# Moving attention visits and value copies inside a fused attention and feed-forward kernel

## The chip, the cores and the metric

The kernel runs on one core of one Trainium2 chip. The metric is the device time in microseconds (us) of one execution. Engines: PE is TensorE (matmuls), DVE is VectorE, ACT is ScalarE, POOL is GpSimd, SP is SyncE, which queues most DMAs here (155 of the 277 issues listed in the trace before). A DMA is a transfer of data that is issued to a queue; PSUM is the memory that this kernel's matmuls write to, in the banks that its plans name. A profile is one traced execution; its times count from the span's start, and the span is 1.7 us shorter than the device time of the same run. The granted clock is the share of TensorE's full speed that the profile shows as granted (1.00 is full). A wait or an idle time is "recorded" when the profile lists it between the end of one instruction and the start of the next.

## The reference

Eight batches of windowed attention (8 heads, 576 positions, width 64, each position sees 32 neighbours on either side), then a feed-forward block (FFN) on the joined heads, token by token.

```python
# attention: q, k, v of (8, 8, 576, 64)
scores = scale * np.matmul(q, k.transpose(0, 1, 3, 2))
mask = np.abs(pos[:, None] - pos[None, :]) <= 32
scores = np.where(mask, scores, -1e9)
attn = softmax(scores)                      # written out in the reference
out = np.matmul(attn, v)
# FFN on x of (4608, 512), w_in (512, 2048), w_out (2048, 512)
h = x @ w_in
g = gelu_tanh(h)
return g @ w_out
```

## The kernel before: the parts that matter

The 4608 tokens are nine blocks of 512. Block t's FFN has a first half (`x @ w_in`, GELU on ACT) and a second half (`g @ w_out`). During the second half, the attention of batch t+1 is slipped between the matmuls: a plan says before which of the matmuls which visit is queued. In a plan, `s` is scores plus exponential, `m` the mask, `v` the weighing of the values (sums `d` and outputs `o`), `x` the normalizing that writes the FFN's input; the digit is a group of two heads (-1: the tail of the batch before, that is its last group) and `@0`, `@1` pick a pair of PSUM banks, where otherwise the banks O and D are used.

```python
PLAN = {4: "s0@0 s1@1 v-1", 26: "m0 x-1", 33: "m1", 34: "s2@0 v0 v1@1", 50: "m2 x0", 56: "x1",
        62: "s3@0 v2", 82: "m3 x2", 91: "s4@1 v3", 105: "m4", 112: "x3"}

def score(b, g, pair):
    ...                                           # matmuls into ps
    pe = ap_.tile([128, 2, w], FP16, name="pe", tag="pe") if g < 4 else ...   # pool of 2 tiles
    nc.scalar.activation(pe, ps[:, :, 0:w], AF.Exp, scale=SCALE)

def mask(b, g, ...):
    nc.vector.tensor_tensor(pe, pe, band..., op=ALU.mult)
def invert(b, g, o, d):                           # 1/d on ACT as exp(-ln d)
    ...
def spread(b, g, o, lt):
    nc.vector.tensor_tensor(xT[...], o[...], lt[...], op=ALU.mult)

def pair_v(b, copy, hs=slice(0, H)):              # values also on the other 64 partitions
    V = Vs[b % 2]
    copy(V[64:128, 4:8, hs, :], V[64:128, 0:4, hs, :])
    copy(V[0:64, 4:7, hs, :], V[0:64, 1:4, hs, :])
```

From block 1 on, the second half is a Winograd product: seven products of 16 matmuls of 256 columns. After each 16, DVE copies or adds the result, and by the program a later product that accumulates in the same bank comes after that (no such wait of PE is recorded in the trace before):

```python
if n == 0:   nc.vector.tensor_copy(M1, py)
elif n == 1: nc.vector.tensor_tensor(U2, py, M1, op=ALU.add)
...
```

DVE runs its instructions in the order in which they are queued (in block 4 a mask whose input was ready at 181.60 us started at 183.65, after the addition queued before it). It also forms four weight differences (`combine`, 1.2 us each): two late in block 0 (`c` in its plan), two in block 1 at matmuls 17 and 33. Batch 2's values are copied by `pair_v` with a DMA from GpSimd's queue, and batch 1's by GpSimd itself.

The softmax here doesn't subtract the row's maximum and nothing guards it: scores larger than these inputs give would overflow.

## Time and profile before

| | before |
|---|---|
| device time, median of 3 runs | 320.15 us (319.9 to 321.78) |
| span of the profiled execution | 317.5 us |
| PE busy | 294.2 us |
| start of block 1's FFN | 62.2 us |
| block 1, start to start of block 2 | 37.6 us |
| blocks 2 to 6 together | 159.6 us |
| rest (blocks 7 and 8) | 58.1 us |

The stages are read from the timeline of PE: an FFN's first half begins where matmuls with `w_in` begin. PE is recorded as busy 93% of the span, so the places to look at are the few where PE waits. The prediction shows those lines.

### The profile page before, as it was taken

What the parts mean: (1) busy time and instruction counts of PE and PEld (TensorE: products, weight loads), DVE (VectorE), ACT (ScalarE), POOL (GpSimd) and SP (SyncE); (2) the same over time, 40 slices, a digit from 0 to 9 for tenths busy, and PEclk for the clock granted to TensorE, in tenths of its full rate; (3) what the DMA queues carried; (4) which work ended last, traced back from release to release, by engine and by line L of the source; (5) the groups of instructions that cost most, each with busy time, mean ns of one, the idle gap of its engine ahead of it and who ended that gap; (6) DMA issues with size and microseconds to landing.
All of it is one profiled execution on the core that took longest, in us unless ns stands there. A gap on an engine that the chain in (4) does not pass through costs nothing.

```text
span 317.5 us, 7161 instructions
## 1 busy us (share of the span) xinstructions
PE 294.2 (93%) x2883; PEld 184.0 (58%) x2883; DVE 191.2 (60%) x421; ACT 185.1 (58%) x283; POOL 109.2 (34%) x169
## 2 busy tenths in 40 slices
PE   6779997999499998999999999999999999999994
PEld 2444543446376467646764676467646764684483
DVE  4674585695648655865576567756775653542352
ACT  1557555567255786478647864786478647805600
POOL 3657459172405800480049004810340033007000
PEclk9989999999789999999999999999999999999998
DMA  6999998989995999399969994999392013004013
GB/s 200 249 351 368 378 316 235 247 132 143 250 170 137 181 228 200 107 148 179 242 140 182 205 213 115 176 200 224 77 213 53 2 34 102 2 0 132 2 33 99
DMA packets 117407, 52.90 MB, mean 167 GB/s; under 512 B 97935, under 2 KB 109967, under 8 KB 117374
## 3 DMA queue, kind: packets, MB, share of 16 engines
q1 hardware_dynamic: 84617, 39.66, 55.6%
q0 software_dynamic: 31824, 11.61, 30.3%
q10 hardware_dynamic: 933, 1.18, 1.1%
q8 instruction: 22, 0.36, 0.5%
q14 instruction: 11, 0.09, 0.1%
HBM read 36.70 MB, written 9.44 MB: 145 GB/s over the span
## 4 chain that ended last, share of the span: by engine, by line
PE 61%; DMA 17%; DVE 8%; ACT 5%; SPq 5%; POOL 2%; issue 1%; DVEq 0%; POOLq 0%
PE mm L544 24%; PE mm L449 16%; PE ph L449 13%; DMA wst<-in_moe_w_in_dram 3%; DMA vr<-in_v_dram 3%; DMA KT<-k 3%; DMA V<-V 3%; DMA qr<-in_q_dram 2%; DVE pe L369 2%; PE mm L515 2%; DMA V<-in_v_dram 2%; ACT pe L363 2%; PE ps_o L388 2%; SPq L133 2%; SPq L142 2%
## 5 line engine op out<-in xcount | busy, mean ns | idle before, releaser
L449 PEld LDWEIGHTS <-w_in 128*128 128x128 f16 x576 | 56.1, 98 | 66.2 <-issue 1.4
L505 POOL DMA_DIRECT2D out_dram<-y x77 | 46.3, 609 | 122.0 <-DVE y L573 121.5
L449 PE MATMUL mm<-xT,w_in 128*128 128x512 f16 x320 | 78.0, 379 | 0.2 <-DVE xT L411 0.2
L457 ACT ACTIVATE gT<-mm 128x512 f16<-128x512 f32 x80 | 47.6, 599 | 44.8 <-PE mm L449 44.2
L449 PE MATMUL ph<-xT,w_in 128*128 128x512 f16 x256 | 64.1, 379 | 0.7 <-ACT gT L457 0.7
L489 DVE TENSOR_TENSOR s<-gT 128x512 f16<-128x512 f16 x64 | 26.9, 420 | 45.4 <-ACT gT L457 45.4
L544 PEld LDWEIGHTS <-s 128*128 128x128 f16 x512 | 49.6, 98 | 6.0
L363 ACT ACTIVATE pe<-ps_s 128x960 f16<-128x960 f32 (+1 forms) x32 | 30.6, 976 | 37.7 <-PE ps_s L355 20.8
L544 PE MATMUL mm<-t,s 128*128 128x256 f16 x376 | 44.7, 273 | 0.0
L457 ACT ACTIVATE gT<-ph 128x512 f16<-128x512 f32 x64 | 36.2, 602 | 12.5 <-PE ph L449 12.4
L544 PEld LDWEIGHTS <-gT 128*128 128x128 f16 x384 | 36.7, 100 | 7.2
L544 PE MATMUL mm<-w_out,gT 128*128 128x256 f16 x256 | 34.2, 281 | 0.0
L402 ACT ACTIVATE lt<-lt 128x480 f32<-128x480 f32 (+3 forms) x40 | 23.5, 587 | 1.3
L388 PEld LDWEIGHTS <-V 128*64 128x64 f16 x520 | 15.5, 115 | 13.1 <-issue 5.9
L172 POOL DMA_DIRECT2D V<-in_v_dram x24 | 22.2, 949 | 1.2 <-DMA out_dram<-y 1.2
L89 ACT ACT_TABLE_LOAD x17 | 21.8, 1283 | 1.1 <-PEq L797 0.8
L369 DVE TENSOR_TENSOR pe<-pe,band 128x960 f16<-128x960 f16 (+1 forms) x32 | 21.7, 679 | 1.0 <-ACT pe L363 1.0
L401 ACT ACTIVATE lt<-ps_d 128x480 f32<-128x480 f32 (+3 forms) x32 | 17.5, 548 | 4.2 <-PE ps_d L382 3.8
L559 DVE COPY y<-mm 128x512 f32<-128x512 f32 x8 | 5.5, 691 | 20.3 <-PE mm L544 20.3
L515 PE MATMUL mm<-w_out,gT 128*128 128x512 f16 x64 | 15.6, 380 | 1.5 <-DVE yo L519 1.2
L544 PE MATMUL mm<-t,gT 128*128 128x256 f16 x128 | 16.3, 273 | 0.0
L355 PE MATMUL ps_s<-QT,KT 64*64 64x128 f16 (+3 forms) x648 | 14.9, 215 | 1.5 <-DVE KT L297 0.7
(85 smaller groups left out, 303.2 us busy)
## 6 DMA issues: line engine op xcount, KB each, us to landing
kr<-in_k_dram SPq DMA_DIRECT2D x32, 256.0 KB, 5.3
qr<-in_q_dram SPq DMA_DIRECT2D x6, 1024.0 KB
wst<-in_moe_w_in_dram SPq DMA_DIRECT2D x3, 1024.0 KB, 12.6
wst<-in_moe_w_out_dram SPq DMA_DIRECT2D x3, 1024.0 KB
V<-in_v_dram POOLq DMA_DIRECT2D x24, 128.0 KB, 7.1
qr<-in_q_dram SPq DMA_DIRECT2D x8, 256.0 KB
vr<-in_v_dram SPq DMA_DIRECT2D x16, 128.0 KB, 5.7
V<-V SPq DMA_DIRECT2D x5, 256.0 KB
```

The lines of the kernel that those rows point to most:

```text
L89: nc.scalar.add_instruction(mybir.InstLoadActFuncSet(name=nc.get_next_instruction_name(), act_func_set_id=which, ins=[], outs=[]))
L172: nc.gpsimd.dma_start(V[:, c, :, :], v[b, :, 128 * c:128 * c + 128, :].rearrange("h p d -> p h d"))
L363: nc.scalar.activation(pe, ps[:, :, 0:w], AF.Exp, scale=SCALE)
L369: nc.vector.tensor_tensor(pe, pe, m.rearrange("k (o j) p -> k o j p", o=1).broadcast_to(list(pe.shape)), op=ALU.mult)
L388: nc.tensor.matmul(o[64 * h:64 * h + 64, cols].rearrange("d (j p) -> d j p", j=4)[:, :, p0 - q0:p1 - q0], Vs[b % 2][:, slot, 2 * pr + h, : ...
L402: nc.scalar.activation(lt[:, 0:n], lt[:, 0:n], AF.Exp, scale=-1.0)
L449: nc.tensor.matmul(ph, w_in16[:, dc, fc * 128:fc * 128 + 128], xT[:, dc, t * 512 % RING:t * 512 % RING + 512], start=(dc == 0), stop=(dc = ...
L457: nc.scalar.activation(gTs[t][:, fc, :], phs[fc], AF.Gelu_apprx_tanh)
L489: nc.vector.tensor_tensor(dst, x, y, op=op)
L505: (eng or turn_about[0] if t == NT - 1 else eng or nc.gpsimd).dma_start(out_v[b, j, q0 + p:q0 + p + e, cols], yo[m:m + e, cols])
L515: nc.tensor.matmul(pys[t4], gTs[0][:, fc, t4 * 128:t4 * 128 + 128], w_out16[:, fc, :], start=new, stop=(fc == NF - 1))
L544: nc.tensor.matmul(pys["apart"][:, 0:256] if apart else py[:, blk, :], lhsT, wino[w][:, f, :], start=(new and i % (8 if one else 16) == 0) ...
```

## The change

The intent: let masks and normalizings run on DVE before the output additions they used to queue behind, so that PE finds them ready; take the value copies of batches 1 and 2 from GpSimd and from a DMA to DVE; keep a third tile for the exponentials; and reorder the first attention (before block 0), where PE waits 1.49 and 0.46 us for DVE's copies of the values. Cut to its core:

```diff
-PLAN = {4: "s0@0 s1@1 v-1", 26: "m0 x-1", 33: "m1", 34: "s2@0 v0 v1@1", 50: "m2 x0", 56: "x1",
-        62: "s3@0 v2", 82: "m3 x2", 91: "s4@1 v3", 105: "m4", 112: "x3"}
+PLAN = {4: "s0@0 s1@1 v-1", 16: "m0 m1 x-1", 33: "s2@0 v0@1 v1", 36: "m2", 44: "x0", 50: "x1",
+        62: "s3@0 v2", 66: "m3", 75: "x2", 91: "s4@1 v3", 105: "m4", 112: "x3"}
-PLAN_0 = {0: "w0 w1 m0", 10: "s-1@0 s1@1", 15: "m-1", 16: "w2 m1", 20: "s2@1 v-1 v0@0", 24: "w3 x-1 x0 m2", ...
+PLAN_0 = {0: "w0 w1 m0", 10: "s1@1 s-1@0", 14: "m1", 16: "w2 m-1", 18: "s2@1 v-1", 24: "w3 m2",
+          28: "d0 x-1", 31: "s3@1 v0@0", 36: "d1", 38: "m3 x0 d2", 41: "v1 v2@1", 45: "d3", 48: "x1 t4", ...
+    pep = ctx.enter_context(tc.tile_pool(name="pep", bufs=3))     # tiles of the exponentials
...   # head: values of heads 6, 7 loaded and cast before the first half weight
...   # first attention: scores of all groups earlier, weighings later, dummy matmuls moved
-                        pair_v(1, nc.gpsimd.tensor_copy, ...)     # batch 1, on GpSimd
+                elif kind == "d":                                 # batch 1, on VectorE
+                    pair_v(b, nc.vector.tensor_copy, slice(2 * g, 2 * g + 2))
-                    trans_tails(1, <bank pair S1>)
+                    trans_tails(1, <bank O>)                      # kind "t"
-        if t == 1:
-            pair_v(unpaired.pop(), nc.gpsimd.dma_start)           # batch 2, a DMA
+            if t == 1 and i == 20:
+                pair_v(unpaired.pop(0), nc.vector.tensor_copy)    # batch 2, on VectorE
```

(Output tiles of block 0 rearranged to make room.) In block 0's plan, `w` is a cast of a quarter of w_out, `d` the value copy of one pair of heads, `t` the transposes of batch 1's tails.

More of the change, by code (lines that the diff above doesn't have):

```diff
@@ L42 @@
         ("S1", "T1", True), ("A22", "T4", False), ("S4", "B22", False)]
-PLAN = {4: "s0@0 s1@1 v-1", 26: "m0 x-1", 33: "m1", 34: "s2@0 v0 v1@1", 50: "m2 x0", 56: "x1",
-        62: "s3@0 v2", 82: "m3 x2", 91: "s4@1 v3", 105: "m4", 112: "x3"}
+PLAN = {4: "s0@0 s1@1 v-1", 16: "m0 m1 x-1", 33: "s2@0 v0@1 v1", 36: "m2", 44: "x0", 50: "x1",
+        62: "s3@0 v2", 66: "m3", 75: "x2", 91: "s4@1 v3", 105: "m4", 112: "x3"}
 TURN_0 = {10: 0, 12: 1, 14: 2, 15: 3}
-PLAN_0 = {0: "w0 w1 m0", 10: "s-1@0 s1@1", 15: "m-1", 16: "w2 m1", 20: "s2@1 v-1 v0@0", 24: "w3 x-1 x0 m2",
-          30: "s3@1 v1", 36: "m3 x1", 42: "v2 v3@0", 48: "t4 x2", 51: "x3 c1", 56: "s4@1", 57: "c2 m4"}
+PLAN_0 = {0: "w0 w1 m0", 10: "s1@1 s-1@0", 14: "m1", 16: "w2 m-1", 18: "s2@1 v-1", 24: "w3 m2",
+          28: "d0 x-1", 31: "s3@1 v0@0", 36: "d1", 38: "m3 x0 d2", 41: "v1 v2@1", 45: "d3", 48: "x1 t4",
+          50: "x2", 51: "v3@0", 53: "c1", 57: "x3", 58: "s4@1", 59: "c2 m4"}
 ORDER_0 = ([(t4, 4 * w + i) for w in range(4) for t4 in (0, 1)
@@ L99 @@
     stage = ctx.enter_context(tc.tile_pool(name="stage", bufs=5))
-    yp = ctx.enter_context(tc.tile_pool(name="yp", bufs=3))
+    yp = ctx.enter_context(tc.tile_pool(name="yp", bufs=2))
     psM = ctx.enter_context(tc.tile_pool(name="psM", bufs=1, space=PSUM))
@@ L209 @@
     vs(4, 5)
+    vs(6, 7)
     wi = [load_w_in(0, stage_w(), 0, 2)]
-    vs(6, 7)
     load_w_in(0, wi[0], 2, 4)
@@ L217, with spin @@
     nc.vector.memset(idle, 0.0)
-    def spin(n, width, score=False):
-        ps = psS.tile([128, 2, 512], FP32, name="spin2", tag="S0")[:, 0, :] if score else \
+    def spin(n, width, pair=None):
+        ps = psS.tile([128, 2, 512], FP32, name="spin2", tag=f"S{pair}")[:, 0, :] if pair is not None else \
             psO.tile([128, 512], FP32, name="spin", tag="O")
@@ L312, in cast_and_turn @@
         qr, kr, qt, kt = raws[b]
-        qt16 = hp.tile([16, NPAIR, 4, 2, 64], FP16, name="qt16")
+        qt16 = hp.tile([16, NPAIR, 4, 2, 64], FP16, name="qt16", tag="qt16")
         kt16 = hp.tile([64, NPAIR, 2, 64], FP16, name="kt16", tag="t16")
@@ L360, in score @@
         w = 4 * n * len(prs)
-        pe = ap_.tile([128, 2, w], FP16, name="pe", tag="pe") if g < 4 else \
+        pe = pep.tile([128, 2, w], FP16, name="pe", tag="pe") if g < 4 else \
             tailp.tile([128, 2, w], FP16, name="pet")
@@ L517, in ffn_out_0 @@
         if fc == NF - 1:
-            yo = yp.tile([128, 512], FP32, name="yo", tag="yo")
+            if t4 == 0:
+                pys["yo"] = hp.tile([128, 2, 512], FP32, name="yo2", tag="qt16")
+            yo = pys["yo"][:, t4, :] if t4 < 2 else yp.tile([128, 512], FP32, name="yo", tag="yo")
             nc.vector.tensor_copy(yo, pys[t4])
@@ L601 @@
     cast_v(0, 2)
+    cast_v(0, 3)
     cast_w(wi[0], w_in16[:, :, 0:512], 0, (0, 1))
-    cast_v(0, 3)
     cast_w(wi[0], w_in16[:, :, 0:512], 0, (2, 3))
@@ L625 @@
     score(0, 0, 0)
-    spin(2, 512)
+    spin(2, 512, 1)
     pt = turn(1)
@@ L629 @@
     mask(0, 0)
-    spin(4, 512)
+    spin(4, 512, 1)
     score(0, 1, 1)
-    cast_vt(0)
-    spin(2, 512)
     pt = turn(2)
     trans_out(0, 2, pt)
+    cast_vt(0)
+    mask(0, 1)
+    spin(4, 512, 0)
+    score(0, 2, 0)
     paired(0)
-    mask(0, 1)
+    spin(3, 512, 1)
     weighed(0)
-    score(0, 2, 0)
+    mask(0, 2)
+    pt = turn(3)
+    trans_out(0, 3, pt)
     spread(0, 0, *ods[0])
-    spin(5, 512)
+    spin(4, 512, 1)
+    score(0, 3, 1)
     paired(1)
+    spin(2, 512, 0)
     weighed(1)
-    pt = turn(3)
     paired(2)
-    trans_out(0, 3, pt)
-    mask(0, 2)
-    spin(3, 512, score=True)
-    score(0, 3, 1)
+    mask(0, 3)
+    weighed(2)
     spread(0, 1, *ods[1])
-    weighed(2)
-    mask(0, 3)
+    ffn_in(0, 0, 0, 2)
     paired(3)
-    ffn_in(0, 0, 0, 2)
     spread(0, 2, *ods[2])
@@ L738 @@
                         cast_v(1, 0)
-                        pair_v(1, nc.gpsimd.tensor_copy, slice(0, 2))
                     if g == 3:
@@ L742 @@
                             cast_v(1, pr)
-                            pair_v(1, nc.gpsimd.tensor_copy, slice(2 * pr, 2 * pr + 2))
                         cast_vt(1)
@@ L747 @@
                 elif kind == "t":
-                    pt = psS.tile([128, 2, 8, 128], FP16, name="pt", tag="S1")
-                    trans_tails(1, pt[:, 0])
+                    trans_tails(1, psO.tile([128, 8, 128], FP16, name="pt", tag="O"))
                 elif kind == "c":
```

## The prediction

> **What bounds the kernel now.** I read the page first: busy shares, then the slices, then the list of what TensorE (PE) waited for, then the timeline around each of those waits.
>
> ```profile
> PE 294.2 (93%) x2883; PEld 184.0 (58%) x2883; DVE 191.2 (60%) x421; ACT 185.1 (58%) x283; POOL 109.2 (34%) x169
> ...
> PE   6779997999499998999999999999999999999994
> ...
> PEclk9989999999789999999999999999999999999998
> DMA  6999998989995999399969994999392013004013
> ```
>
> PE is 93% busy of 317.5 us: 23.3 us of idle is all that a reordering can win, plus what the clock loses after idle (the slices with 7 and 8 in the clock row). One slice is about 7.9 us. From stage to stage, by a table of windows, the idle is 7.3 us before 40 us, 2.4 us between 40 and 56, 4.4 us between 80 and 88, 0.5 to 0.9 us per later 20 us, and about 4.3 us at the end, where nothing is changed. The list of PE's waits names the owners:
>
> ```profile
> PE ps_o L388 <- DMA V<-V: 4.0, 1, 4.0
> PE ps_od L382 <- DVE pe L369: 2.8, 5, 0.9
> ...
> PE ps_d L382 <- DVE pe L369: 1.2, 3, 0.8
> PE mm L515 <- DVE yo L519: 1.2, 1, 1.2
> ...
> PE ps_od L388 <- POOL V L180: 0.7, 1, 0.7
> ```
>
> The largest is a single wait in the first Winograd stage (token block 1): the values of batch 2 are copied to the other half of the partitions by a GpSimd-queued DMA, and PE needs the copy. In the timeline:
>
> ```profile
> 77.91 0.55 POOL L180 DMA_DIRECT2D V<-V  x1
> ...
> 82.97 1.22 DVE L479 TENSOR_TENSOR t<-w_out,t 128x2048 f16<-128x2048 f16 x1
> ...
> 86.30 0.53 PE L388 MATMUL ps_o<-pe,V 128*64 128x64 f16 x12 [4.04 <-DMA V<-V]
> ...
> 87.57 3.05 PE L544 MATMUL mm<-w_out,gT 128*128 128x256 f16 x14
> ```
>
> The reader is to see that the copy takes over 8 us from issue to use, and that the 14 matmuls afterwards took 3.05 us (other stages: 1.70 us): the clock had gone to 0.50 and came back near 90.4 us, which costs about 4.1/2 = 2.0 us more.
>
> The second owner recurs once in each of blocks 2 to 6 (0.86, 0.24, 0.56, 0.57, 0.57 = 2.8 us). Block 4 as an example:
>
> ```profile
> 183.05 0.68 DVE L557 TENSOR_TENSOR y<-mm,y 128x512 f32<-128x512 f32 x1
> ...
> 183.65 0.65 DVE L369 TENSOR_TENSOR pe<-pe,band 128x960 f16<-128x960 f16 x1
> 183.82 0.97 ACT L363 ACTIVATE pe<-ps_s 128x960 f16<-128x960 f32 x1 [1.28 <-PE ps_o L388]
> 184.35 0.39 PE L382 MATMUL ps_od<-pe,ones 128*64 128x480 f16 x2 [0.56 <-DVE pe L369]
> ```
>
> The second mask (L369) stands behind the output addition (L557) on in-order VectorE, though its exponentials were ready at 181.6; PE waits for it. And the third group's exponential (183.82) had to wait for PE to finish reading the first group's tile: only two tiles for the exponentials.
>
> [...] The trace agrees at 83.6 to 90.4 us (granted 0.50 after a 4.0 us wait), but also shows 0.50 from about 15.4 to 18.5 us after an idle of only 1.49 us amid small matmuls, so a shorter wait is not surely safe. [...] The value copies of batch 0 agree:
>
> ```profile
> L179 DVE COPY V<-V x4: 291/558/673, 13.4 to 22.6; 64x512 f16<-64x512 f16 x4
> L180 DVE COPY V<-V x4: 282/284/285, 13.9 to 23.2; 64x384 f16<-64x384 f16 x4
> ```
>
> The 291 ns one ran while GpSimd was idle, the slow ones beside its casts. [...] a third tile is part of the change.
>
> **The change, part by part.**
>
> Part 1, blocks 2 to 6. Both masks move to matmul 16, behind the copy of product 0 and ahead of the addition of product 1. By block 4's clock: copy ends 181.4, masks 181.95 and about 182.5 (0.65 us each, slightly overlapped), the normalizing of the previous tail follows at 182.55 to 183.1 as before, the addition at 183.7. PE reaches the second group's weighing near 183.3 to 183.5, so its mask is ready: wait 0. It now uses the output bank that the normalizing frees at 183.1: ready in time. The addition is needed by matmul 48, near 186: ready. With the third tile the third exponential can start near 183.0. The later moves (third mask at 36, fourth at 66, normalizings at 44, 50, 75) land behind inputs that are ready and ahead of needs; the 0.16 us wait on a normalizing in block 4 goes too. Gain 2.8 + 0.2 = 3.0 us. No instruction is added here.
>
> Part 2, block 1. The DMA copy of batch 2's values becomes two VectorE copies (64x2048 and 64x1536) at matmul 20. [...] VectorE's order there is: copy of product 0 (79.03 to 79.72), two masks (to 80.85), normalizing of the tail (its input comes at 80.85; to 81.45), weight difference L479 (1.22, to about 82.6), the two copies (to about 83.8), then the addition. PE gets to the values near 81.65 (it starts the scores at matmul 33, about 80.8, and needs 0.35 + 0.25 + 0.2 us). So a wait of 83.8 - 81.65, about 2.2 us, stays, now for VectorE instead of the DMA. Block 1 idled 4.39 us between 80 and 88; it saves 2.2 us. The half-clock stretch costs 2.0 us now; with a 2.2 us gap I give it 40%, so 1.2 us saved in the mean. Gain 3.4 us.
>
> Part 3, block 0. The value copies of batch 1 leave GpSimd (4 pairs of 0.61 + 0.58 to 0.8 us, about 5.3 us) for VectorE (4 x about 0.55 us uncontended = 2.2 us, up to 0.9 each beside GpSimd's casts). VectorE is about 70% busy there, so there is room. Gone: the 0.69 us wait on GpSimd's copy and the 1.19 us wait on the output copy behind a mask. New by my hand schedule: about 0.8 us around the w_out casts (that weight arrives at 43.5 whatever PE does), 0.3 us at the first weighing, 0.5 us at the third. Old idle about 2.4, new about 1.8: gain 0.6 us.
>
> Part 4, the first attention. Reordered so that PE need not wait for value casts; heads 6 and 7 of the values are loaded before the first half weight.
>
> ```profile
> 20.11 0.88 POOL L270 CAST V<-vr 128x512 f16<-128x512 f32 x1 [1.31 <-DMA vr<-in_v_dram]
> ...
> 24.08 2.27 POOL L198 CAST w_in<-wst 128x512 f16<-128x512 f32 x4 [1.08 <-DMA wst<-in_moe_w_in_dram]
> ```
>
> I expect the FFN to start without a break near 21.8 instead of 24.1. But the second weight lands at 24.08 and its third cast ends near 25.8, and DMA is already full (305 to 400 GB/s from 16 us on), so column 4 and 5 can end near 26.7 instead of 27.54. Gain 0.85 us of the 2.3.
>
> Sum: 3.0 + 3.4 + 0.6 + 0.85 = 7.85 us, and I add 0.4 us for the half clock at 15 to 18 us and small waits that go with the reordering: 8.2 us. 320.15 - 8.2 = about 312.0.
>
> **Rivals.** (a) The wait in block 1 only changes owner: VectorE's copies come after a 1.22 us weight difference, and with a slow copy (half speed, or GpSimd issuing the next value loads at the time, 0.9 us each) they end near 85, wait 3.4 us, clock lost again. Then block 1 saves about 1 us and the time is 314.5. For it: the in-order queue and GpSimd's four issues between 78.4 and 82; against it: those issues end before the copies begin. (b) Loading is the bound up to 48 us (DMA row at 9, and the chain that ended last runs through loads of weights, queries and values up to 46.2 us). Then parts 3 and 4 gain nothing: 313.5. For it: the arrival times; against it: the two waits of 1.19 and 0.69 us were not for a DMA. (c) Blocks 2 to 6 gain less because a moved mask or normalizing now makes an output addition late and PE waits for a bank: 1 to 2 us back, 313.5. Against it: my schedule leaves over 2 us to matmul 48. (d) Better than the sum: the clock stays full in block 1 and the start gains its whole 2.3 us: 309.
>
> **Range and chances.** (a), (b) and (c) are partly independent; two of them together give about 315.5. So 312.0, 308.5 to 315.3 for 8 in 10. The line of 2% is 313.75; I put 0.72 below it. That nothing or less comes of it is remote, since the 2.8 us of mask waits and the 4.0 us wait are plainly removed or shortened: slower 0.01.
>
> **What would show it.** Right: the list of PE's waits has no "DVE pe" entry for blocks 2 to 6; the "DMA V<-V" entry is replaced by one for VectorE's copy of about 2 us; the value copies take about 0.7 and 0.55 us; PE's idle from 120 to 260 us falls from 3.6 to under 1 us (one 0.56 us wait on a key transpose may stay); GpSimd's busy time falls by about 5 us; block 1's FFN starts about 1.5 to 2 us earlier than 62.2. Wrong: the copy's wait over 3 us with the clock at 0.50, new waits on L411 or L557 in every block, or the start of block 1 unmoved.

## The result, and the profile after

The change is faster: 311.53 us (309.7 to 313.42, 4 runs) against 320.31 us (4 runs), ratio 0.9719, 95% interval 0.9663 to 0.9774. (A run counts as slow when it lies over 1.5% above the fastest of the same kernel, and slow runs are left out of every ratio.) A ratio here and below is the mean time of one kernel's fast runs over that of the other's fast runs of the same rounds, so it isn't quite the ratio of the medians.

The profiled execution after, from the page: busy shares, then PE and its granted clock by slices.

```profile
PE 291.7 (94%) x2886; PEld 181.8 (59%) x2886; DVE 193.6 (63%) x431; ACT 185.4 (60%) x283; POOL 102.7 (33%) x159
...
PE   7879889799699999998999999999999999999994
...
PEclk9999999999979999999999999999999999999999
```

PE's idle fell from 23.3 to 309.7 - 291.7 = 18.0 us, that is by 5.3 us, but the span fell by 7.8 us: some of the gain isn't in the recorded idle at all. By stages of the two traces:

| stage | before | after | difference | predicted |
|---|---|---|---|---|
| up to block 0's second half | 40.59 | 39.71 | -0.88 | -0.85 |
| block 0's second half | 21.57 | 23.59 | +2.02 | -0.6 |
| block 1 | 37.58 | 34.59 | -2.99 | -3.4 |
| blocks 2 to 6 | 159.63 | 153.70 | -5.93 | -3.0 |
| blocks 7, 8 | 58.13 | 58.11 | -0.02 | 0 |

The list of what PE waited for, after (columns: total us, times, longest):

```profile
PE ps_od L390 <- DVE V L182: 3.1, 3, 2.4
PE pt L283 <- DVE xT L413: 1.4, 1, 1.4
...
PE mm L517 <- DVE w_out L200: 1.2, 1, 1.2
PE ps_s L357 <- DMA KT<-k: 0.9, 1, 0.9
```

The first line sums three waits; the longest, 2.4 us, is block 1's. The mask waits of blocks 2 to 6 are gone; the only recorded wait left in these blocks is the 0.9 us one, for a key transpose (0.56 us before; it differs from execution to execution). The DMA wait has become a 2.4 us wait for DVE's value copy. And two waits that the prediction did not have, or had smaller, are in block 0: the tail transposes (L283) and a w_out cast.

The signs that the prediction named came true but one: the idle of PE from 120 to 260 us fell from 3.6 to 0.89 us and GpSimd's busy time by 6.5 us, but block 1's FFN starts at 63.30 us, 1.1 us later than before and not 1.5 to 2 us earlier.

**Blocks 2 to 6: why 5.9 us and not 3.0.** In these blocks the recorded idle of PE fell from 3.92 to 0.89 us, that is by the 3.0 us predicted; the other 2.9 us were never recorded as idle. Block 4's PE timeline before: sums of the first weighing (start, duration), then its outputs; the second weighing's line stands in the prediction, at 184.35 us.

```profile
182.91 0.39 PE L382 MATMUL ps_d<-pe,ones 128*64 128x480 f16 x2
183.28 0.50 PE L388 MATMUL ps_o<-pe,V 128*64 128x96 f16 x14
```

The same in block 4 after:

```profile
178.97 0.39 PE L384 MATMUL ps_od<-pe,ones 128*64 128x480 f16 x2
179.19 0.40 PE L390 MATMUL ps_od<-pe,V 128*64 128x96 f16 x14
179.42 0.37 PE L384 MATMUL ps_d<-pe,ones 128*64 128x480 f16 x2
```

Here both masks come before the addition, in one entry:

```profile
177.49 1.22 DVE L371 TENSOR_TENSOR pe<-pe,band 128x960 f16<-128x960 f16 x2
...
179.22 0.68 DVE L561 TENSOR_TENSOR y<-mm,y 128x512 f32<-128x512 f32 x1
```

Read the starts, not the idle column. After, from the first outputs to the second sums takes 179.42 - 179.19 = 0.23 us; before, 184.35 - 183.28 = 1.07 us. So that wait cost 0.84 us, while the timeline records 0.56. From sums to outputs it was 0.37 us before and is 0.22 now: 0.15 us lost with no wait recorded. A weighing late in the block lost 0.32 us with 0.16 recorded (sums to outputs: 192.52 to 193.07 before, 187.68 to 187.91 after). Together 1.31 of the 1.36 us by which the second half of block 4 shortened (18.07 to 16.71 us), with 0.72 recorded. A matmul's recorded end hides this: where nothing waits, the next matmul starts well before it (after: the sums end at 178.97 + 0.39 = 179.36, the outputs start at 179.19), an overlap of 0.17 us, and a wait is counted only from that end on (before: 183.28 + 0.50 + 0.56 = 184.34, where the second sums start).

**Block 1.** DVE's copies and PE's wait after:

```profile
83.73 0.69 DVE L181 COPY V<-V 64x2048 f16<-64x2048 f16 x1
84.44 0.55 DVE L182 COPY V<-V 64x1536 f16<-64x1536 f16 x1
...
85.05 0.54 PE L390 MATMUL ps_od<-pe,V 128*64 128x64 f16 x12 [2.36 <-DVE V L182]
...
86.31 2.80 PE L548 MATMUL mm<-w_out,gT 128*128 128x256 f16 x15
```

The copies take 0.69 and 0.55 us, about the 1.2 us that the prediction's schedule left for them (82.6 to 83.8, the estimate), and begin at 83.73, behind two masks, a normalizing and a weight difference, 6.6 us after the start of the second half as in the prediction's schedule (82.6 - 75.97). Then 15 matmuls take 2.80 us, where block 4 needs 1.81: the clock fell again (granted 0.50 from about 85.0 to 88.4 us).

**Block 0.** DVE and PE after, around the tail transposes:

```profile
57.17 0.69 DVE L523 COPY yo<-mm 128x512 f32<-128x512 f32 x1 [1.47 <-PE mm L517]
57.78 0.65 DVE L413 TENSOR_TENSOR xT<-ps_o,lt 128x480 f16<-128x480 f32 x1
58.57 0.38 PE L283 MATMUL pt<-idn,t 128*128 128x128 f16 x4 [1.44 <-DVE xT L413]
```

The transposes now write bank O. The second normalizing (57.78) must first read bank O, and it is queued on DVE behind an output copy that waits for PE's matmul 47. DVE idles 1.47 us for PE, and PE then 1.44 us for DVE. Recorded idle in block 0's second half rose from 2.38 to 3.74 us.

### The profile page after: what moved, and what is told of

The parts are those of the page before. It is cut to its first block, busy times and chain, and to the rows that moved or that the text cites.

```text
span 309.7 us, 7146 instructions
## 1 busy us (share of the span) xinstructions
PE 291.7 (94%) x2886; PEld 181.8 (59%) x2886; DVE 193.6 (63%) x431; ACT 185.4 (60%) x283; POOL 102.7 (33%) x159
## 4 chain that ended last, share of the span: by engine, by line
PE 75%; DMA 12%; SPq 6%; DVE 3%; ACT 1%; issue 1%; POOL 1%; DVEq 0%
PE mm L548 31%; PE mm L451 19%; PE ph L451 15%; DMA wst<-in_moe_w_in_dram 3%; DMA wst<-in_moe_w_out_dram 3%; SPq L144 3%; DMA KT<-k 3%; DMA qr<-in_q_dram 3%; PE ps_s L357 3%; PE ps_d L384 2%; PE mm L517 2%; PE ps_o L390 2%; SPq L135 2%; PE ps_od L390 1%; SPq L191 1%
## 5 line engine op out<-in xcount | busy, mean ns | idle before, releaser
L404 ACT ACTIVATE lt<-lt 128x480 f32<-128x480 f32 (+3 forms) x40 | 23.5, 587 | 1.3
L371 DVE TENSOR_TENSOR pe<-pe,band 128x960 f16<-128x960 f16 (+1 forms) x32 | 20.6, 660 | 2.6 <-ACT pe L365 2.6
L357 PEld LDWEIGHTS <-KT 64*64 64x64 f16 x648 | 10.3, 106 | 11.1 <-issue 7.1
```

What stands on the lines that cost most here:

```text
L357: nc.tensor.matmul(ps[64 * half:64 * half + 64, h, 4 * n * r:4 * n * r + 4 * n].rearrange("k (j p) -> k j p", j=4)[:, :, p0 - q0:p1 - q0], ...
L404: nc.scalar.activation(lt[:, 0:n], lt[:, 0:n], AF.Exp, scale=-1.0)
```

## The experiments

All twelve kernels were correct. Each was timed in five rounds (six runs of each kernel, four of the first). The kernel before ran in the same rounds: medians 319.85 us for the first four kernels, 320.3 for the next four and 320.68 for the last four.

### One part at a time

First, each part alone, put into the kernel before.

**Only the new plan of blocks 1 to 6** (with its third tile).

```diff
-PLAN = {... 26: "m0 x-1", 33: "m1", 34: "s2@0 v0 v1@1", 50: "m2 x0", ...}
+PLAN = {... 16: "m0 m1 x-1", 33: "s2@0 v0@1 v1", 36: "m2", 44: "x0", ...}
+    pep = ... bufs=3
```

> Before, with only the new visit plan of blocks 1 to 6 and its third tile for the exponentials (and the output tiles rearranged to make room). My theory after comparing traces: blocks 2 to 6 gain 6.0 us together (1.3 to 1.6 each, block 3 less for its key transpose), twice what the recorded waits said, because a wait costs PE about 0.2 to 0.3 us more than the recorded idle; block 1 keeps its 4 us wait for the DMA copy. So 314.2 us, ratio 0.981. Rival, the prediction's own sizing: recorded idle is all that is lost, gain 3.0, 317.2 us, ratio 0.991.

Measured: 312.15 us, ratio 0.9758 (0.9716 to 0.98). In its trace blocks 2 to 6 take 152.88 us, 6.75 less than before, and block 1 keeps its wait for the DMA:

```profile
87.03 0.53 PE L389 MATMUL ps_od<-pe,V 128*64 128x64 f16 x12 [4.87 <-DMA V<-V]
```

The rival that recorded idle is all that is lost (ratio 0.991) falls. So does, narrowly, the number expected (0.981): blocks 2 to 6 gained somewhat more than the 6.0 us of the theory, and the timing shows about 2 us more than expected. This part alone is most of the whole gain.

**Only batch 2's value copy on DVE**, old plan.

```diff
-            pair_v(unpaired.pop(), nc.gpsimd.dma_start)      # before block 1's second half
+            if t == 1 and i == 20: pair_v(unpaired.pop(0), nc.vector.tensor_copy)
```

> Before, with only batch 2's value copy on VectorE at matmul 20 of block 1, old plan. Theory: the 4.0 us wait becomes two of about 1.4 us each (value copy and first mask, then second mask, all queued on VectorE), and the clock may fall: block 1 saves 1.5 to 3.5 us, ratio 0.989 to 0.995. Rival: most of block 1's gain needs the moved masks, so saving under 1 us.

Measured: 315.83 us, ratio 0.9872 (0.9833 to 0.9911), a little better than the band expected, though the interval reaches into it; the rival (under 1 us) falls. Block 1 takes 33.96 us, 3.62 less than before, and blocks 2 to 6 are unchanged (159.69). The wait is now split, on PE:

```profile
83.75 0.39 PE L382 MATMUL ps_d<-pe,ones 128*64 128x480 f16 x2 [1.45 <-DVE pe L369]
...
85.38 0.39 PE L382 MATMUL ps_od<-pe,ones 128*64 128x480 f16 x2 [0.65 <-DVE pe L369]
```

PE waits for masks that now stand behind the copies. The clock stayed full here (a mean of 1.00 over the execution), so part of the 3.62 us is the half clock of the trace before, by estimate about 2 us (half of the 4.06 us from 86.30 to 90.36 at 0.50).

**Only the first attention** (with the earlier load and cast of value heads 6 and 7).

```diff
-    wi = [load_w_in(0, stage_w(), 0, 2)]
     vs(6, 7)
+    wi = [load_w_in(0, stage_w(), 0, 2)]
...
+    # scores of all groups ahead of the weighings, as in the change
```

> Before, with only the reordered first attention and the earlier load of value heads 6 and 7. Theory: weights arriving set the pace, so block 0's FFN ends only 0.9 us earlier, and block 0's second half, paced by w_out arrivals, gives part of it back: -0.4 to -0.9 us, ratio 0.997 to 0.999. Rival: the whole 2 us by which the first FFN matmuls start earlier survive, ratio 0.994.

Measured: 318.99 us, ratio 0.9996 (0.995 to 1.0041). No effect is seen, to within 0.5%; the 2 us rival (0.994) lies outside, if narrowly, and the small gain expected (0.997 to 0.999) can be neither seen nor excluded.

**Only block 0's part**: its plan, batch 1's copies on DVE, tail transposes in bank O, third tile.

```diff
+PLAN_0 = {... as in the change ...}
-                        pair_v(1, nc.gpsimd.tensor_copy, ...)
+                elif kind == "d": pair_v(b, nc.vector.tensor_copy, ...)
```

> Before, with only block 0's part: the new plan of block 0, batch 1's value copies on VectorE, tail transposes in another bank, third exponential tile. Theory: this part makes the kernel slower by 2.0 us (new waits of 1.2 us for a w_out cast and 1.4 us for the tail transposes' bank), ratio 1.006. Rival: block 0 is slower in the full change only because the first attention ran earlier and block 0 waits for arrivals either way; then alone it costs 0 to 1 us.

Measured: 319.82 us, ratio 1.0003 (0.9965 to 1.0042). The 2.0 us loss that the first pair of traces showed is outside this interval, if narrowly (1.006); a loss up to 1.3 us isn't. The 1.19 and 1.44 us waits are there in its trace.

### Repairs of the change

Second, edits of the changed kernel that each take away one wait.

**Value copies at matmul 5**, where DVE idles 0.67 us for product 0 in the trace of the change, instead of 20.

```diff
-            if t == 1 and i == 20:
+            if t == 1 and i == 5:
```

> After, with batch 2's value copies queued at matmul 5 of block 1 instead of 20, so VectorE makes them while it waits for product 0. Theory: the 2.36 us wait goes, and with it the half clock after it: block 1 saves 2.4 + 0.3 + 1.5 to 1.7 = about 4.2 us, 307.3 us, ratio to before 0.959. Rival: the clock falls anyway or a new wait for the first mask takes over: 2.5 us or less, 309 us.

Measured: 309.1 us, ratio 0.9644 (0.9605 to 0.9684). In its trace the 2.36 us wait is gone, the clock is full (1.00 from 80.5 to 100.5 us), and a new one has come later in block 1:

```profile
80.71 0.92 DVE L181 COPY V<-V 64x2048 f16<-64x2048 f16 x1
81.65 0.55 DVE L182 COPY V<-V 64x1536 f16<-64x1536 f16 x1
...
89.75 0.42 PE L390 MATMUL ps_o<-pe,V 128*64 128x96 f16 x14 [0.94 <-DVE xT L413]
```

Block 1's second half went from 20.77 to 18.22 us: 2.55 of the 4.2 us hoped for, the number of the rival, though by another wait than it named. The expectation did not have the normalizing that now stands behind two weight differences on DVE. The first copy took 0.92 us here, where GpSimd had started to issue a DMA 0.25 us before it (at 80.46 us, 0.69 us long), against 0.69 us in the traces of the change and of the copy alone, where GpSimd did nothing beside it.

**The second normalizing of block 0 at 47.**

```diff
-PLAN_0 = {... 48: "x1 t4", ...
+PLAN_0 = {... 47: "x1 t4", ...
```

> After, with block 0's second normalizing queued one matmul earlier (47 instead of 48), ahead of an output copy on VectorE. Theory: the 1.44 us wait of the tail transposes for their bank goes: -1.4 to -1.7 us, 310.0 us. Rival: the next thing in line (output copy of token tile 2, or the last normalizings) takes it over: under 0.5 us.

Measured: 310.33 us, ratio 0.9695 (0.9655 to 0.9735). The 1.44 us wait is gone from its trace and no other takes its place there. Against the change's 0.9719 the time isn't clearly different.

This run gave something unplanned. Its block 1 is the change's, with the same wait (2.35 us), but here the clock stayed full (granted 1.00). Windows of the change around that wait, then of this kernel (length of the window; PE, PEld, DVE, ACT, POOL busy, where PEld is PE's weight loading; then granted clock, DMA share, GB/s):

```profile
83.12:85.12 2.00, 0.07 (x2) 0.07 (x4) 1.97 (x4) 0.23 (x1) 0.00 (x0) 0.96 1.31 249
85.12:87.12 2.00, 2.00 (x32) 1.49 (x33) 2.00 (x3) 1.47 (x3) 0.00 (x0) 0.50 1.34 281
```

```profile
83.18:85.18 2.00, 0.07 (x4) 0.07 (x6) 1.97 (x4) 0.23 (x1) 0.00 (x0) 1.00 1.23 288
85.18:87.18 2.00, 2.00 (x41) 1.74 (x42) 2.00 (x3) 1.62 (x3) 0.00 (x0) 1.00 1.35 268
```

Block 1's second half took 20.77 us in the one and 19.26 in the other: the clock costs 1.5 us, and whether it is lost after such a wait differs between executions.

Windows of 0.2 us place the moments of change. In the trace before:

```profile
15.20:15.40 0.20, 0.20 (x2) 0.06 (x1) 0.20 (x1) 0.20 (x1) 0.20 (x2) 0.67 0.90 294
...
18.60:18.80 0.20, 0.20 (x4) 0.20 (x3) 0.00 (x0) 0.20 (x1) 0.20 (x1) 0.80 1.01 273
...
83.40:83.60 0.20, 0.00 (x0) 0.00 (x0) 0.20 (x1) 0.00 (x0) 0.00 (x0) 0.84 1.47 305
...
90.20:90.40 0.20, 0.20 (x3) 0.14 (x2) 0.00 (x0) 0.00 (x0) 0.00 (x0) 0.59 1.59 157
```

Taking each mean as a mix of 1.00 and 0.50, the clock fell at 15.27 and 83.54 us and came back at 18.68 and 90.36. The distances, 3.41, 64.86 and 6.82 us, are 1, 19 and 2 times 3.41 in this one trace. Windows read in the same way put the clock at 0.50 from 84.97 to 88.38 us in the trace of the change, from 86.42 to 89.82 in that of the plan alone and from 85.65 to 89.06 in that of the cast first: 3.4 us in each. In block 1 it fell each time while PE was still waiting: 1.3 us into the wait in the trace before (4.04 us), 4.3 us into it with the plan alone (4.87 us), 2.3 us in the change (2.36 us) and 1.9 us with the cast first (2.35 us). What decides is not shown: no run moved a wait alone, and there is no plain threshold (early in the trace before, the clock fell 1.0 us after the end of a wait of 1.49 us among small matmuls, and in this kernel it held through 2.35 us).

**The third w_out cast ahead of the second mask.**

```diff
-PLAN_0 = {... 14: "m1", 16: "w2 m-1", ...
+PLAN_0 = {... 14: "w2 m1", 16: "m-1", ...
```

> After, with block 0's third w_out cast queued on VectorE ahead of the second mask. Theory: the 1.19 us wait at 45.4 us shrinks by about 0.7 us, and half of that survives: -0.3 to -0.7 us. Rival: the weight's arrival (43.4 us) bounds it, or w_out's last part does a little later: 0.

Measured: 311.28 us, ratio 0.9716 (0.968 to 0.9752). The 1.19 us wait is gone from its trace, waits of 0.37 us for another w_out cast and 0.30 us for a mask appear, and the time doesn't tell it from the change. Inconclusive at this size. (The clock was lost in block 1 of this trace, in a wait of 2.35 us: 0.50 granted from 86.17 to 88.17 us.)

**All three edits.**

> After, with all three edits (copy at 5, normalizing at 47, cast first). If independent: -4.2 - 1.5 - 0.5 = -6.2 us, about 305.4 us, ratio to before 0.953, the best of all. Rival: the gains overlap, 307.

Measured: 307.92 us, ratio 0.9611 (0.9574 to 0.9649): faster than the change, but 2.5 us short of the full sum; 0.94 us of this is the new wait in block 1.

### Without the head parts, and the best versions

**The change without its head**: first attention and block 0 as before.

```diff
 PLAN, pep, value copies of batch 2 at 20: as in the change
-everything before block 1: as in the change
+everything before block 1: as in the kernel before
```

> The full change without its two head parts (first attention and block 0 as before): new plan, third tile, batch 2's value copies on VectorE at matmul 20. Theory: the head parts gain nothing, their block 0 costs about 1.4 us once the arrival of w_out is taken out, so this is as fast as the full change or faster: 310 to 311.5 us, ratio 0.967 to 0.972; in its trace block 1 starts 23.9 us after the first w_out arrives (25.3 in the full change). Rival: the head parts are worth the 0.9 us that the first trace pair shows before block 0: 312.4 us, ratio 0.975.

Measured: 310.11 us, ratio 0.9653 (0.9612 to 0.9693). As fast as the change (0.9719) or faster. The rival, head parts worth 0.9 us (0.975), falls. Its block 1 second half took 19.25 us, with the clock full (1.00) after a 2.35 us wait.

The single traces differ in the head whatever the kernel: with the head as before, block 1 starts at 61.0 to 63.6 us. The loads don't arrive at the same time in every execution (w_out's first quarter at 37.5 to 39.7 us), and counted from that arrival the spread is 1.0 us. The mark is the cast on GpSimd that is released by w_out's first quarter; before and after:

```profile
38.12 1.35 POOL L198 CAST w_out<-wst 128x512 f16<-128x512 f32 x2 [2.83 <-DMA wst<-in_moe_w_out_dram]
```

```profile
38.02 1.16 POOL L200 CAST w_out<-wst 128x512 f16<-128x512 f32 x2 [2.85 <-DMA wst<-in_moe_w_out_dram]
```

So I count from there to the start of block 1's FFN, start column minus start column:

| head | us from w_out's first arrival to block 1, by run |
|---|---|
| as before (before, plan only, copy only, old head, two tiles, best with old head) | 24.0, 23.9, 23.9, 23.0, 23.9, 23.1 |
| new first attention, old block 0 | 24.5 |
| new block 0, old first attention | 25.4 |
| both, as in the change (the change, copies at 5) | 25.3, 25.8 |
| both, normalizing at 47; cast first | 24.7; 25.1 |
| both, with all three edits (these; best with new head) | 23.5, 23.2 |

By this count block 0's part costs some 1.5 to 2 us, and the two block 0 edits together take that away, without a gain beyond the old head. It is one trace of each kernel, so a reading and not a timing; and the timing of block 0's part alone allowed a loss of 1.3 us at most. What the timings show is no gain from the head parts.

**Two tiles instead of three**, in the kernel with the old head. (In the full change two tiles would make the engines wait in a circle in block 0, by its plan and not by a run: exponential 2 for weighing 0, this for the copy d0, this on DVE behind mask 2, which needs exponential 2.)

```diff
-    pep = ... bufs=3
+    pep = ... bufs=2
```

> As the kernel with the old head and the copies at 20, but two tiles for the exponentials instead of three. Theory: the masks' place, not the third tile, removes the waits; with two tiles the third exponential starts 0.5 us later and that is hidden: within 1 us of it (ratio to before at most 0.003 more), and no wait over 0.3 us in blocks 2 to 6. Rival[...]: too few buffers made the gap, so about half of the 6 us is lost again, ratio 0.977 or more.

Measured: 310.41 us, ratio 0.9689 (0.966 to 0.9717), against 0.9653; the intervals overlap, and the difference of 0.0036 is a little over what I had allowed. Blocks 2 to 6 took 153.52 us (152.76 with three), and the only wait recorded in them is 0.71 us for a key transpose. Block 4 with two tiles, third exponential and third mask:

```profile
178.90 0.97 ACT L364 ACTIVATE pe<-ps_s 128x960 f16<-128x960 f32 x1 [0.92 <-PE ps_od L389]
...
179.90 0.66 DVE L370 TENSOR_TENSOR pe<-pe,band 128x960 f16<-128x960 f16 x1 [0.73 <-ACT pe L364]
```

ACT waits 0.92 us for PE to give the tile back, and DVE 0.73 us for ACT, and PE for nobody. So the third tile was not what closed the gap on PE; the new plan was, and the traces put it down to the masks' place in DVE's queue (the plan moves other visits too, and no run moved the masks alone).

**Best with the old head**: copies at 5 and block 1's fourth weight difference, first needed by the product that starts at matmul 80, at 51 instead of 33.

```diff
-                          33: (T4, B21, T2)})
+                          51: (T4, B21, T2)})
```

> Old head, new plan, third tile, value copies at matmul 5, and the fourth weight difference of block 1 at matmul 51 instead of 33, so that VectorE reaches the normalizing sooner. Theory: block 1 needs 17.2 us for its second half (before 23.8), blocks 2 to 6 save 6.0 to 6.7: 307.5 us, ratio 0.960, as good as the all-edits kernel with the new head (307.9). Rival: the 0.94 us wait only moves to another instruction: 308.7 us.

Measured: 306.6 us, ratio 0.9553 (0.952 to 0.9585). Block 1's second half took 17.08 us (before 23.77), with no wait in it; better than expected.

**Best with the new head**: all three edits, and the same move of the weight difference.

> New head with all three edits of before (copies at 5, normalizing at 47, cast first), and the fourth weight difference of block 1 at matmul 51. Theory: the 0.94 us wait of block 1 goes with its hidden 0.25: 306.8 us, ratio 0.958. Rival: no change against 307.9 us.

Measured: 305.97 us, ratio 0.9535 (0.9504 to 0.9566), from five fast runs, better than expected; one slow run of 312.09 is left out (with it the median is 306.23). Both take about 4.5% less than the kernel before, and by their ratios to it (0.955 and 0.954 against 0.972) some 1.8% less than the change. Between the two the intervals overlap: the new head, once repaired, is worth nothing that these runs can tell.

## Why the prediction was right or wrong

The time (312.0 against 311.53) and the class were right. The sum was right by luck: two of its terms were wrong in opposite directions, by 2.9 and 2.6 us.

1. **Part 1, blocks 2 to 6: mechanism right, size wrong.** The masks were ready, the addition was in time, no new wait came. The term "2.8 + 0.2 = 3.0 us" was mis-sized: it added up recorded idle. Measured: 5.93 us in the pair of traces, of which 3.03 is recorded idle, and 6.75 with this part alone (its trace lacks the 0.9 us wait for the key transpose). The working shown above for block 4 finds the rest in starts that came late without an idle entry. Of its secondary reasoning, the two tiles as a cause were wrong for this gap: with two tiles the gap is gone as well (153.52 us for blocks 2 to 6). And "0.5 to 0.9 us per later 20 us" misreads the table of windows: of the seven from 120 to 260 us, two have 0.10 us.
2. **Part 2, block 1: right.** A wait of 2.2 us for DVE was predicted, 2.36 was found, and the copies took 0.69 and 0.55 us where its schedule left about 1.2 us (the estimate; no trace had shown copies of these sizes). Rival (a) happened in its clock part only: the clock was lost in the profiled execution, to which I had given 40%. Recorded idle fell by 2.19 us (4.55 to 2.36), as predicted. So this execution saved 2.99 us where 3.4 were expected in the mean; in the run where the clock held, block 1's second half was 1.5 us shorter still. One reading was off: the clock was not lost "after a 4.0 us wait" but at 83.54 us, 1.3 us into it.
3. **Part 3, block 0: wrong.** The step "Old idle about 2.4, new about 1.8: gain 0.6 us" failed. The two waits it named are gone, but my hand schedule moved the tail transposes without asking who holds bank O: the 1.44 us wait wasn't in it, and the one for the w_out cast was 1.19 us. Block 0 lost 2.0 us in the pair of traces, 1.5 to 2 us when counted from the arrival of w_out; alone, the part changed nothing that a timing shows (1.3 us lost at most).
4. **Part 4, the first attention: the number was met in the trace (0.88 against 0.85) by luck, and it wasn't a gain.** Alone it gave a ratio of 0.9996. The step that failed is "Gain 0.85 us of the 2.3", an earlier end of block 0's first half: over all fourteen traces its second half starts at 39.2 to 42.1 us with the old first attention and at 39.7 to 42.3 with the new one, and the trace of the change happens to be the earliest of its seven. That parts 3 and 4 gain nothing is what rival (b) said, and the runs show it; that loading is the cause is supported by the count from w_out's arrival, but no run changed the loads.
5. **The added 0.4 us** for the half clock at 15 to 18 us: the clock was full there in the trace after (1.00 up to 84.8 us), but no run shows a gain from it.

The parts alone multiply to 0.9758 x 0.9872 x 0.9996 x 1.0003 = 0.963, against 0.9719 for the change and 0.9653 without the head parts. The product is near the last. What the head parts together cost in time is therefore some 0 to 2 us; the timings leave it open, and only the count from w_out's arrival points at 1.5 us or more.

Open as well: why the arrival of w_out differs by 2.3 us between executions (37.5 to 39.7 us after the start), and what decides whether the clock falls in a wait of about 2.3 us (waits of 2.36 and 2.35 us lost it in two traces, with 0.50 granted afterwards, and waits of 2.35 us kept it in two others, at 1.00).

## What to carry to other kernels

Price a wait on TensorE by the distance between the starts of matmuls, compared with the same pair of matmuls where nothing waits, and not by the recorded idle: here the idle held only half of the loss (3.03 of 5.93 us in blocks 2 to 6). On an engine that works in order, as DVE did here, ask for each moved instruction what now stands ahead of it and what that waits for; moving 1.2 us of copies from a busy place to one where VectorE idled 0.67 us and nothing behind was urgent took away a 2.4 us wait (and left one of 0.9 us later on). And where the start of a stage moves with arriving data (w_out's arrival moved by 2.3 us between these executions), single traces can't tell gains or losses of a few tenths to two us: count from the arrival before calling either.
